# Second feed-forward: blocks run further ahead, the last 512 tokens end chunk by chunk, GpSimd drains early

## The chip, the cores and the metric

The kernel runs on one core of a Trainium2 chip. The core has five engines that run side by side: TensorE (PE in the profile; its weight loads are listed apart as PEld), VectorE (DVE), ScalarE (ACT), GpSimd (POOL) and SyncE (SP). They share an on-chip memory of 128 partitions; TensorE writes into eight banks of a separate accumulation memory, called `bk[0]` to `bk[7]` here, and VectorE and ScalarE read them. The metric is the device time of one execution in microseconds (us), as the median of several runs.

## The reference, cut to what matters

Three layers follow one another: a gated linear attention over 2 x 768 tokens, a mixture of eight experts of which each token takes one, and a second feed-forward with the Mish activation over all 1536 tokens. The change is in the last.

```python
def _moe2_ref(x, w_in, w_out) -> np.ndarray:      # x: 1536 x 384, w_in: 384 x 2048
    h = x @ w_in
    sp = np.where(h > 20.0, h, np.log1p(np.exp(np.minimum(h, 20.0))))
    g = h * np.tanh(sp)
    return (g @ w_out).astype(np.float32)
```

## The kernel before, in words

The kernel keeps its tokens sorted by expert. In the second feed-forward the 2048 hidden features are 16 groups of 128 (`m` from 0 to 15) and the tokens three groups of 512 (`w0` of 0, 512, 1024). One pair of the two is a **block** `(w0, wd, m)`. For a block, `f1` makes the first product in one bank, `sigma` and `cosine` turn it on ScalarE into the Mish factor (sigmoid, arctangent, sine), `gated` on VectorE multiplies and splits the result into a high part `gh` and a low part `gl`, and `f2` makes the second product. Every product is made of three matmuls (high by high, low by high, high by low), so `f1` is 9 matmuls of 512 columns (3 slices of the 384 inputs) and `f2` 12 matmuls of 384 columns: three for each **chunk** of 128 tokens, summed up over `m` in that chunk's bank. Bank 0, 1, 4 and 5 take first products in turn (`h2_rot`), banks 2, 3, 6 and 7 the sums of four chunks (`o_rot`).

The blocks stand in the list `steps`: a **first pass** with `m` below `MA` = 10 for all three token groups (blocks 0 to 29) and a **second pass** with the other six (from block 30). At the end of a group in the first pass `f_keep` copies the four sums to memory; at its end in the second pass `f_out` adds the kept sum on VectorE, and `f_scatter` puts an indirect DMA on GpSimd's queue that writes the chunk's 128 rows to their places in the output. There are twelve such scatters. Earlier in the program GpSimd issues 24 more indirect DMAs, twelve into a table of tokens (`tab`) and twelve into their order (`toks`), so 36 in all.

The order on each engine is the order of the code. One round of the main loop is `f_head(n)` (the first product of block n; then in `f_mish` ScalarE's work on it, the adds of chunks that are full, and `gated` for the pair of blocks finished a round ago), then `f_tail(n)` (the second product of block n - 3, `LAG2`), then at most one scatter. ScalarE works on two blocks at a time so that it loads its function tables twice a pair. In the last token group of the kernel before, `m` = 15 is split into two halves of 256 tokens, with a pairing of its own, and the last two blocks' second products are interleaved:

```python
        elif i >= len(steps) - 2:

            b, w0 = steps[-3], steps[i][0] // 128
            tail = [(b, w0), (b, w0 + 1), (steps[i], w0), (steps[i], w0 + 1)]
            if i == len(steps) - 1:
                tail[1:3] = tail[2:0:-1]
            for b, c in tail:
                f2(b, [c])
                if full:
                    f_out(full.pop()[1])
                    f_scatter(1)
```

`gh` and `gl` lie side by side in a buffer from `big_tile` (three buffers in turn). The weights of the second feed-forward lie as `whi` and `wlo` in the pools `wr_p[0]` (`m` from 0 to 7) and `wr_p[1]` (the rest), eight buffers of each tag in each pool.

When the last block is out, each engine reads a flag (`slow_i`, L1324), branches past a slow path (L1325), GpSimd waits for its scatters to land and updates their semaphores (INC_SWDGE_SEM), and all engines meet after a drain (L1543).

Of the kernel before, what the change touches and what calls it, by code (L numbers as in the profile page):

```python
# [11 lines left out]
F32R = mybir.dt.float32r  # L12
# [11 lines left out]
def kernel(  # L24
# [18 lines left out]
    nc = tc.nc  # L43
    ctx.enter_context(tc.manual_schedule())
    B, H, S, D = q.shape
    NT, DM = out.shape
# [13 lines left out]
    MF2 = FF2 // 128  # L60
# [4 lines left out]
    PW = 768  # L65
    ATT = 4
    W2N = 512
# [12 lines left out]
    wr_p = {0: main.enter_context(tc.tile_pool(name="wr0", bufs=8))}  # L80
# [71 lines left out]
    MA = 10  # L152
# [23 lines left out]
    whi, wlo, wst_t, cvt_t = {}, {}, {}, {}  # L176
# [163 lines left out]
    def w_second(e, m):  # L340
        i = NP1 * e + m // 2 * 2 + 1
        return [w[i][:, m % 2 * DM:(m % 2 + 1) * DM] for w in (whi, wlo)]


    with ExitStack() as actx:
# [626 lines left out]
        i = NTILE - 1  # L972
# [32 lines left out]
    def big_tile():  # L1005
        return fp.tile([128, 1024], F32, tag="big", name="big", bufs=3)
# [94 lines left out]
        nc.vector.tensor_reduce(out=pk, in_=po, axis=AX.X, op=ALU.add)  # L1101
        nc.vector.tensor_tensor(out=pos_i, in0=pk, in1=rs_all, op=ALU.add)

    g_t, o_t, h2_t, p_t, g_b = {}, {}, {}, {}, [None]
    h2_rot, o_rot = [0, 1, 4, 5], [2, 3, 6, 7]
    h2_n, o_n = [0], [0]

# [31 lines left out]
    def gated(b):  # L1139
        w0, wd, m = b  # L1140
        g = p_t.pop(b)
        if w0 % W2N == 0:
            g_b[0] = big_tile().bitcast(F32R)
        gh, gl = (g_b[0][:, o + w0 % W2N:o + w0 % W2N + wd] for o in (0, W2N))
        nc.vector.tensor_tensor(out=g, in0=g, in1=h2_t.pop(b), op=ALU.mult)  # L1145
        nc.vector.tensor_copy(out=gh, in_=g)
        nc.vector.tensor_tensor(out=gl, in0=g, in1=gh.bitcast(F32), op=ALU.subtract)  # L1147
        g_t[b] = (gh, gl)

    def f2(b, chunks=None):  # L1150
        w0, wd, m = b
        gh, gl = g_t[b]
        wh, wl = w_second(E, m)
        for c in range(w0 // 128, (w0 + wd) // 128) if chunks is None else chunks:
            if m in (0, MA):
                o_t[c] = bk[o_rot[o_n[0] % len(o_rot)]][:, 0:DM]
                o_n[0] += 1
            ts = slice(c * 128 - w0, (c + 1) * 128 - w0)
            for n, (a, b_) in enumerate(((gh, wh), (gh, wl), (gl, wh))):
                nc.tensor.matmul(  # L1160
                    out=o_t[c], lhsT=a[:, ts], rhs=b_,
                    start=(m in (0, MA) and n == 0), stop=(m in (MA - 1, MF2 - 1) and n == 2),
                )
            if m in (MA - 1, MF2 - 1):
                full.append((m, c))

    acc_c, ready, full = {}, [], []
# [14 lines left out]
    def f_out(c):  # L1182
        ob = acc_c.pop(c)
        nc.vector.tensor_tensor(out=ob, in0=o_t.pop(c), in1=ob, op=ALU.add)  # L1184
        ready.append((c, ob))

    def f_scatter(n):
        for c, ob in ready[:n]:
            scatter(out, srt[:, c:c + 1], ob, NT, "out")
        del ready[:n]  # L1190

    steps = []
    for ms in (range(MA), range(MA, MF2)):
        for w0 in range(0, NT, W2N):
            for m in ms:
                wd = W2N // 2 if w0 + W2N == NT and m == MF2 - 1 else W2N
                steps += [(w0 + o, wd, m) for o in range(0, W2N, wd)]
    LAG2 = 3
    NS = len(steps)
    pairs_ = [(n, n + 1) for n in range(0, NS - 3, 2)] + [(NS - 3,), (NS - 2, NS - 1)]  # L1200
    last_of = {p[-1]: p for p in pairs_}
    due = []

    def at(n):
        return steps[n] if 0 <= n < NS else None


    def f_mish(n):
        late = (n - EARLY) // 2 if n > EARLY else -9
        if n % 2 == 0:  # L1210
            late_high(late - 1)
            sigma(at(n)) if at(n) else None
            late_size(late)
        elif at(n):
            sigma(at(n))
        if n in last_of:
            bs = [at(i) for i in last_of[n]]
            cosine(bs)
        for m, c in full:
            (f_out if m >= MA else f_keep)(c)  # L1220
        full.clear()
        now = list(due)
        due.clear()
        if n in last_of:
            due.extend(bs)
        for b in now:
            gated(b)
        if n % 2:
            late_low(late - 2)
            late_join(late - 1)  # L1230
            late_load(late + LATE_AHEAD - 1)
        conv_to(E * MF - EARLY + n + 3 + LEAD)

    def f_head(n):
        if at(n):
            f1(at(n))
        f_mish(n)

    def f_tail(n):
        i = n - LAG2  # L1240
        if 0 <= i < len(steps) - 3:
            f2(steps[i])
        elif i >= len(steps) - 2:

            b, w0 = steps[-3], steps[i][0] // 128
            tail = [(b, w0), (b, w0 + 1), (steps[i], w0), (steps[i], w0 + 1)]
            if i == len(steps) - 1:
                tail[1:3] = tail[2:0:-1]
            for b, c in tail:
                f2(b, [c])  # L1250
                if full:
                    f_out(full.pop()[1])
                    f_scatter(1)

    EARLY = LAG2
    CVT_END = 45
# [57 lines left out]
        late_load(i)  # L1314
    f_mish(EARLY)
    f_tail(EARLY)
    for n in range(EARLY + 1, NS + LAG2):
        f_head(n)
        f_tail(n)
        f_scatter(1)  # L1320


    main.close()
    slow = nc.values_load(slow_i[0:1, 0:1], min_val=0, max_val=1)  # L1324
    with tc.If(slow > 0), ExitStack() as sctx:  # L1325
# [71 lines left out]
        for i in range(NTILE):  # L1397
            b, c = divmod(i, NC_B)
# [149 lines left out]
```

## Time and profile before

| | |
|---|---|
| runs | 444.93, 441.98, 444.04 us; median 444.04 us |
| the profiled execution | 442.65 us, of it 440.8 us from the first to the last instruction (the span) |
| TensorE matmul busy | 416.6 us (95% of the span) |
| weight loads / VectorE / ScalarE / GpSimd busy | 377.8 / 326.2 / 331.6 / 61.1 us |
| mean granted TensorE clock | 0.988 of full speed |

All times in the rows below are microseconds from the start of the span unless marked ns. A matmul's duration in the profile includes its way through the pipeline; the distance between the starts of two matmuls is what one costs in a row of them.

### The profile page before, as it was taken

What the parts mean: (1) busy time and instruction counts of PE and PEld (TensorE: products, weight loads), DVE (VectorE), ACT (ScalarE), POOL (GpSimd) and SP (SyncE); (2) the same over time, 40 slices, a digit from 0 to 9 for tenths busy, and PEclk for the clock granted to TensorE, in tenths of its full rate; (3) what the DMA queues carried; (4) which work ended last, traced back from release to release, by engine and by line L of the source; (5) the groups of instructions that cost most, each with busy time, mean ns of one, the idle gap of its engine ahead of it and who ended that gap; (6) DMA issues with size and microseconds to landing.
All of it is one profiled execution on the core that took longest, in us unless ns stands there. A gap on an engine that the chain in (4) does not pass through costs nothing. (4 is left out here: it accounts for less than half of the span.)

```text
span 440.8 us, 8448 instructions
## 1 busy us (share of the span) xinstructions
PE 416.6 (95%) x3139; PEld 377.8 (86%) x3139; DVE 326.2 (74%) x652; ACT 331.6 (75%) x584; POOL 61.1 (14%) x74
## 2 busy tenths in 40 slices
PE   6899989799999999999999999999999999999990
PEld 2787877589999999999988989899899898998980
DVE  7899997689899979988747857967786544543750
ACT  4877995478878777867688788788788677677760
POOL 3143565210100102100000000000000000030302
PEclk9999999899999999999999999999999999999996
DMA  7999752499999999998842121121000000010102
GB/s 233 351 315 351 262 178 76 158 296 263 319 336 339 317 291 290 341 314 249 243 137 66 43 72 36 37 61 49 1 1 0 1 0 0 1 72 1 71 4 75
DMA packets 51566, 68.89 MB, mean 156 GB/s; under 512 B 5500, under 2 KB 41852, under 8 KB 51516
## 3 DMA queue, kind: packets, MB, share of 16 engines
q1 hardware_dynamic: 49596, 63.55, 46.6%
q0 software_dynamic: 1920, 4.73, 3.0%
q8 instruction: 26, 0.43, 0.4%
q14 instruction: 24, 0.20, 0.1%
HBM read 56.65 MB, written 11.61 MB: 155 GB/s over the span
## 5 line engine op out<-in xcount | busy, mean ns | idle before, releaser
L1160 PE MATMUL bk<-whi,big 128*128 128x384 f32 x384 | 106.5, 338 | 1.4 <-DVE x2l L1066 0.8
L329 DVE TENSOR_TENSOR wlo<-st,whi 128x768 fp32r<-128x768 f32 x74 | 69.9, 953 | 17.7 <-ACT whi L323 17.0
L1145 DVE TENSOR_TENSOR p<-p,bk 128x512 f32<-128x512 f32 (+1 forms) x49 | 33.0, 673 | 58.8 <-ACT p L1137 56.1
L1160 PEld LDWEIGHTS bk<-whi,big 128*128 128x128 f32 x384 | 70.5, 188 | 4.5 <-DVE x2l L1066 1.1
L323 ACT ACTIVATE whi<-st 128x768 fp32r<-128x768 f32 x74 | 61.7, 843 | 6.6 <-DMA st<-in_w_dram 6.5
L1160 PE MATMUL bk<-wlo,big 128*128 128x384 f32 x192 | 64.9, 338 | 0.0
L1131 ACT ACTIVATE p<-bk 128x512 f32<-128x512 f32 (+1 forms) x49 | 28.8, 591 | 39.5 <-PE bk L1119 38.2
L1056 PE MATMUL bk<-hl,whi 128*128 128x240 f32 x192 | 52.9, 276 | 0.0
L1056 PE MATMUL bk<-hh,wlo 128*128 128x240 f32 x192 | 52.7, 275 | 0.0
L1056 PE MATMUL bk<-hh,whi 128*128 128x240 f32 x192 | 52.7, 274 | 0.0
L101 POOL DMA_INDIRECT out_dram<-acc,srt x12 | 11.7, 973 | 236.7 <-DVE acc L1184 234.3
L1119 PE MATMUL bk<-x2l,whi 128*128 128x512 f32 (+1 forms) x147 | 41.8, 393 | 0.0
L1119 PE MATMUL bk<-x2h,wlo 128*128 128x512 f32 (+1 forms) x147 | 41.4, 390 | 0.0
L1119 PE MATMUL bk<-x2h,whi 128*128 128x512 f32 (+1 forms) x147 | 41.2, 389 | 0.0
L1160 PEld LDWEIGHTS bk<-wlo,big 128*128 128x128 f32 x192 | 36.0, 188 | 1.7
L1056 PEld LDWEIGHTS bk<-hl,whi 128*128 128x128 f32 x192 | 36.3, 189 | 0.2 <-DVE hl L1044 0.2
L1056 PEld LDWEIGHTS bk<-hh,whi 128*128 128x128 f32 x192 | 36.4, 189 | 0.0
L1056 PEld LDWEIGHTS bk<-hh,wlo 128*128 128x128 f32 x192 | 36.3, 189 | 0.0
L1043 ACT ACTIVATE hh<-bk 128x240 fp32r<-128x240 f32 x64 | 23.5, 366 | 15.5 <-PE bk L1039 15.2
L1039 PE MATMUL bk<-xh,whi 128*128 128x240 f32 x192 | 33.5, 283 | 1.2 <-DVE hl L1044 1.0
L1147 DVE TENSOR_TENSOR big<-p,big 128x512 fp32r<-128x512 f32 (+1 forms) x49 | 33.4, 682 | 1.7
L1119 PEld LDWEIGHTS bk<-x2h,wlo 128*128 128x128 f32 x147 | 27.3, 187 | 6.7
(222 smaller groups left out, 866.1 us busy)
## 6 DMA issues: line engine op xcount, KB each, us to landing
st<-in_w_dram SPq DMA_DIRECT2D x64, 384.0 KB
qn<-in_q_t_dram SPq DMA_DIRECT2D x12, 256.0 KB
kn<-in_k_t_dram SPq DMA_DIRECT2D x12, 256.0 KB
w<-in_w_in_dram SPq DMA_DIRECT2D x6, 512.0 KB
w<-in_w_out_dram SPq DMA_DIRECT2D x6, 512.0 KB
tab<-zero SPq DMA_DIRECT2D x4, 720.0 KB
an<-in_alpha_t_dram SPq DMA_DIRECT2D x11, 256.0 KB
vn<-in_v_n_dram SPq DMA_DIRECT2D x12, 192.0 KB
```

The source lines that it names most:

```text
L101: r = nc.gpsimd.indirect_dma_start(out=dst[:, :], out_offset=bass.IndirectOffsetOnAxis(ap=idx, axis=0), in_=src, in_offset=None, bounds_ch ...
L323: nc.scalar.activation(out=whi[i], in_=w, func=AF.Copy)
L329: nc.vector.tensor_tensor(out=wlo[i], in0=w, in1=whi[i].bitcast(F32), op=ALU.subtract)
L1039: nc.tensor.matmul(out=hps, lhsT=a[:, kk], rhs=b_[:, kk, :], start=(n == 0), stop=(n == 3 * KD - 1))
L1043: nc.scalar.activation(out=hh, in_=hps, func=AF.Relu)
L1056: nc.tensor.matmul(out=y[n], lhsT=a[:, ns], rhs=b_, start=(m == 0 and t == 0 and n % 2 == 0), stop=(m == MF - 1 and t == 2), skip_group_ch ...
L1119: r = nc.tensor.matmul(out=hps, lhsT=a[:, kk], rhs=b_[:, kk, w0:w0 + wd], start=(n == 0), stop=(n == 3 * KD - 1))
L1131: nc.scalar.activation(out=p, in_=h2_t[b], func=AF.Sigmoid, scale=-1.0)
L1145: nc.vector.tensor_tensor(out=g, in0=g, in1=h2_t.pop(b), op=ALU.mult)
L1147: nc.vector.tensor_tensor(out=gl, in0=g, in1=gh.bitcast(F32), op=ALU.subtract)
L1160: nc.tensor.matmul(out=o_t[c], lhsT=a[:, ts], rhs=b_, start=(m in (0, MA) and n == 0), stop=(m in (MA - 1, MF2 - 1) and n == 2),)
```

## The change

It is confined to the second feed-forward's loop. The split of the last `m` goes: there are 48 blocks, all of 512 tokens, paired two by two. From block 34 on `f_tail` lets the second products fall behind by one more block at a time (three times in all), so the lag goes from three blocks to six; each time there is a round without a second product. For blocks of the second pass `gh` and `gl` go into buffers of `wr_p[0]` instead of `big_tile`. After the loop a new function `f_last` makes the second products of the last six blocks (the last token group's whole second pass), ordered by chunk. Two calls `nc.gpsimd.drain()` are added, after rounds 28 and 44.

```diff
     def gated(b):
         w0, wd, m = b
         g = p_t.pop(b)
-        if w0 % W2N == 0:
-            g_b[0] = big_tile().bitcast(F32R)
-        gh, gl = (g_b[0][:, o + w0 % W2N:o + w0 % W2N + wd] for o in (0, W2N))
+        if m >= MA:
+            gh, gl = (wr_p[0].tile([128, PW], F32R, tag=t, name=t)[:, 0:wd] for t in ("whi", "wlo"))
+        else:
+            t = big_tile().bitcast(F32R)
+            gh, gl = t[:, 0:wd], t[:, W2N:W2N + wd]
...
-            for m in ms:
-                wd = W2N // 2 if w0 + W2N == NT and m == MF2 - 1 else W2N
-                steps += [(w0 + o, wd, m) for o in range(0, W2N, wd)]
+            steps += [(w0, W2N, m) for m in ms]
...
+    NL = MF2 - MA
+    NS2 = MA * NT // W2N
+    assert NS % 2 == 0 and NL % 2 == 0 and NL > LAG2
+    pairs_ = [(n, n + 1) for n in range(0, NS, 2)]
...
+    done2 = [0]
+
     def f_tail(n):
...
+        lag = LAG2 + min(max(n - NS2 - 1, 0) // 3, NL - LAG2)
+        if done2[0] <= n - lag:
+            f2(steps[done2[0]])
+            done2[0] += 1
+
+    def f_last():
+        assert done2[0] == NS - NL
+        last = steps[NS - NL:]
+        cs = range(last[0][0] // 128, (last[0][0] + W2N) // 128)
+
+        def part(bs, c, end=False):
+            for b in bs:
                 f2(b, [c])
-                if full:
-                    f_out(full.pop()[1])
-                    f_scatter(1)
+            if end:
+                f_out(full.pop()[1])
+                f_scatter(1)
+
+        for c in cs[:3]:
+            part(last[:-2], c)
+        for c in cs[:2]:
+            part(last[-2:-1], c)
+        for c in cs[:2]:
+            part(last[-1:], c, True)
+        part(last[-2:], cs[2], True)
+        part(last, cs[3], True)
...
-    for n in range(EARLY + 1, NS + LAG2):
+    for n in range(EARLY + 1, NS):
         f_head(n)
         f_tail(n)
         f_scatter(1)
+        if n in (NS - 20, NS - 4):
+            nc.gpsimd.drain()
+    f_mish(NS)
+    f_scatter(NT // 128)
+    f_last()
```

What this does to the order, at three places. On TensorE around round 34 of the kernel before (`bk4` and `bk5` take the first products of blocks 34 and 35, `bk2` is a chunk's sum; `big_4684` and `big_4688` hold the gated blocks 30 and 31):

```order
L1160 MATMUL bk7_90<-whi75_3868,big_4684 128x384
L1119 MATMUL bk4_87<-x2h_1364,whi78_4356 128x512 x3
L1119 MATMUL bk4_87<-x2l_1365,whi78_4356 128x512 x3
L1119 MATMUL bk4_87<-x2h_1364,wlo78_4357 128x512 x3
L1160 MATMUL bk2_85<-whi75_3868,big_4688 128x384
L1160 MATMUL bk2_85<-wlo75_3869,big_4688 128x384
```

and at the same place of the changed kernel:

```order
L1162 MATMUL bk7_90<-whi75_3868,wlo_4686 128x384
L1119 MATMUL bk4_87<-x2h_1364,whi78_4356 128x512 x3
L1119 MATMUL bk4_87<-x2l_1365,whi78_4356 128x512 x3
L1119 MATMUL bk4_87<-x2h_1364,wlo78_4357 128x512 x3
L1119 MATMUL bk5_88<-x2h_1364,whi78_4356 128x512 x3
L1119 MATMUL bk5_88<-x2l_1365,whi78_4356 128x512 x3
L1119 MATMUL bk5_88<-x2h_1364,wlo78_4357 128x512 x3
L1162 MATMUL bk2_85<-whi75_3868,whi_4690 128x384
```

The first product of block 35 follows that of block 34 directly; block 31's second product comes behind both. The same happens at rounds 37 and 40.

On TensorE near the end of the kernel before, where the second product of `m` = 14 (gated block `big_5155`) begins for the last token group, behind that of `m` = 13 (`big_5125`):

```order
L1160 MATMUL bk7_90<-whi77_4150,big_5125 128x384
L1160 MATMUL bk7_90<-wlo77_4151,big_5125 128x384
L1160 MATMUL bk7_90<-whi77_4150,big_5125 128x384
L1160 MATMUL bk2_85<-whi79_4430,big_5155 128x384
L1160 MATMUL bk2_85<-wlo79_4431,big_5155 128x384
L1160 MATMUL bk2_85<-whi79_4430,big_5155 128x384
L1160 MATMUL bk3_86<-whi79_4430,big_5155 128x384
```

and in the changed kernel, where the same product reads `whi_5145` and `wlo_5146`:

```order
L1162 MATMUL bk6_89<-whi77_4150,whi_5097 128x384
L1162 MATMUL bk6_89<-wlo77_4151,whi_5097 128x384
L1162 MATMUL bk6_89<-whi77_4150,wlo_5098 128x384
L1162 MATMUL bk2_85<-whi79_4430,whi_5145 128x384
L1162 MATMUL bk2_85<-wlo79_4431,whi_5145 128x384
L1162 MATMUL bk2_85<-whi79_4430,wlo_5146 128x384
L1162 MATMUL bk3_86<-whi79_4430,whi_5145 128x384
```

Ahead of it there now stand the 36 matmuls of `m` = 10 to 13 for three chunks (`bk2`, `bk3`, `bk6`), all behind the last first product; behind it come 36 more, of which the last 18 are all for the fourth chunk, `bk7`.

On VectorE at the end of the kernel before (two half blocks of `m` = 15, then the four last adds):

```order
L1145 TENSOR_TENSOR p_5153<-p_5153,bk5_88 128x256
L1146 CAST big_5204<-p_5153 128x256
L1147 TENSOR_TENSOR big_5204<-p_5153,big_5204 128x256
L1145 TENSOR_TENSOR p_5183<-p_5183,bk0_83 128x256
L1146 CAST big_5204<-p_5183 128x256
L1147 TENSOR_TENSOR big_5204<-p_5183,big_5204 128x256
L1184 TENSOR_TENSOR acc_4719<-bk2_85,acc_4719 128x384
L1184 TENSOR_TENSOR acc_4719<-bk3_86,acc_4719 128x384
L1184 TENSOR_TENSOR acc_4722<-bk6_89,acc_4722 128x384
L1184 TENSOR_TENSOR acc_4722<-bk7_90,acc_4722 128x384
```

and in the changed kernel:

```order
L1186 TENSOR_TENSOR acc_4398<-bk3_86,acc_4398 128x384
L1186 TENSOR_TENSOR acc_4401<-bk6_89,acc_4401 128x384
L1186 TENSOR_TENSOR acc_4401<-bk7_90,acc_4401 128x384
L1147 TENSOR_TENSOR p_5090<-p_5090,bk4_87 128x512
L1148 CAST whi_5145<-p_5090 128x512
L1149 TENSOR_TENSOR wlo_5146<-p_5090,whi_5145 128x512
L1147 TENSOR_TENSOR p_5123<-p_5123,bk5_88 128x512
L1148 CAST whi_5150<-p_5123 128x512
L1149 TENSOR_TENSOR wlo_5151<-p_5123,whi_5150 128x512
L1186 TENSOR_TENSOR acc_4722<-bk2_85,acc_4722 128x384
L1186 TENSOR_TENSOR acc_4722<-bk3_86,acc_4722 128x384
```

The adds of the middle token group (`acc_4398`, `acc_4401`) now stand directly ahead of the last two gated blocks. On GpSimd the twelve scatters keep their order; one drain stands ahead of the first of them and one behind the third.

## Rows read from the trace of the kernel before

**Rows 1.** The page: span, then busy time, share and instructions of each engine.
```profile
span 440.8 us, 8448 instructions
PE 416.6 (95%) x3139; PEld 377.8 (86%) x3139; DVE 326.2 (74%) x652; ACT 331.6 (75%) x584; POOL 61.1 (14%) x74
```

**Rows 2.** Windows of two rounds: busy time per engine, clock, DMA share, GB/s.
```profile
core 0: us, PE busy (x) PEld busy (x) DVE busy (x) ACT busy (x) POOL busy (x), PEclk, DMA share, GB/s
405.40:413.82 8.42, 8.42 (x44) 7.60 (x44) 5.38 (x10) 6.14 (x9) 1.77 (x2) 1.00 0.06 23
```

**Rows 3.** Timeline of TensorE: start, duration, engine, line, operation, tiles, count.
```profile
409.61 0.85 PE L1119 MATMUL bk<-x2h,whi 128*128 128x512 f32 x3
...
411.71 0.34 PE L1160 MATMUL bk<-whi,big 128*128 128x384 f32 x1
...
413.81 0.86 PE L1119 MATMUL bk<-x2h,whi 128*128 128x512 f32 x3
...
425.21 0.34 PE L1160 MATMUL bk<-whi,big 128*128 128x384 f32 x1
426.14 0.44 PE L1160 MATMUL bk<-whi,big 128*128 128x384 f32 x1 [0.59 <-DVE big L1146]
...
429.34 0.33 PE L1160 MATMUL bk<-whi,big 128*128 128x384 f32 x1
```

**Rows 4.** Timeline of VectorE near the end.
```profile
410.92 1.94 DVE L1184 TENSOR_TENSOR acc<-bk,acc 128x384 f32<-128x384 f32 x4
...
416.34 0.46 DVE L1146 CAST big<-p 128x512 fp32r<-128x512 f32 x1
...
418.70 0.69 DVE L1147 TENSOR_TENSOR big<-p,big 128x512 fp32r<-128x512 f32 x1
...
429.71 0.56 DVE L1184 TENSOR_TENSOR acc<-bk,acc 128x384 f32<-128x384 f32 x1 [0.49 <-PE bk L1160]
```

**Rows 5.** Timeline of GpSimd near the end.
```profile
411.74 0.97 POOL L101 DMA_INDIRECT out_dram<-acc,srt  x1 [19.89 <-DVE acc L1184]
...
428.41 0.97 POOL L101 DMA_INDIRECT out_dram<-acc,srt  x1 [11.86 <-DVE acc L1184]
...
432.24 0.97 POOL L101 DMA_INDIRECT out_dram<-acc,srt  x1 [0.30 <-issue]
```

**Rows 6.** Line L101, GpSimd's scatters, ns min/median/max; landings in 428:433.5, then 386:392.
```profile
L101 POOL DMA_INDIRECT toks<-tokid,pos_i x12: 970/980/1752, 96.2 to 183.7; - x12
L101 POOL DMA_INDIRECT out_dram<-acc,srt x12: 972/973/976, 387.0 to 432.2; - x12
...
DMA to landing us min/median/max: 3.5/3.5/3.5
DMA to landing us min/median/max: 2.8/2.8/2.8
```

**Rows 7.** The kernel's end, L1325 and L1543 (q: an engine's sequencer).
```profile
L1325 POOLq EVENT_SEMAPHORE  x3: 43/43/4280, 431.5 to 435.9; - x3
L1325 POOLq INC_SWDGE_SEM  x1: 900/900/900, 436.0 to 436.0; - x1
...
L1543 SPq DRAIN  x2: 7/10/13, 437.6 to 437.7; - x2
L1543 POOLq DRAIN  x1: 3013/3013/3013, 437.0 to 437.0; - x1
...
L1543 POOLq DRAIN  x2: 40/74/107, 440.2 to 440.5; - x2
```

**Rows 8.** The kernel's start, L1536.
```profile
L1536 POOLq INC_SWDGE_SEM  x1: 31/31/31, 0.2 to 0.2; - x1
...
L1536 POOLq DRAIN  x1: 187/187/187, 0.4 to 0.4; - x1
```

**Rows 9.** Weight loads of two lines, whole span: ns min/median/max, first and last start.
```profile
L1160 PEld LDWEIGHTS bk<-whi,big x384: 186/188/189, 233.7 to 429.2; 128*128 128x128 f32 x192
...
L1056 PEld LDWEIGHTS bk<-hh,wlo x192: 187/189/193, 93.8 to 231.5; 128*128 128x128 f32 x192
```

More of the change, by code (lines that the diff above doesn't have):

```diff
@@ L1102, in sort_places @@
         nc.vector.tensor_tensor(out=pos_i, in0=pk, in1=rs_all, op=ALU.add)
-    g_t, o_t, h2_t, p_t, g_b = {}, {}, {}, {}, [None]
+    g_t, o_t, h2_t, p_t = {}, {}, {}, {}
     h2_rot, o_rot = [0, 1, 4, 5], [2, 3, 6, 7]
@@ L1194 @@
         for w0 in range(0, NT, W2N):
-            for m in ms:
-                wd = W2N // 2 if w0 + W2N == NT and m == MF2 - 1 else W2N
-                steps += [(w0 + o, wd, m) for o in range(0, W2N, wd)]
+            steps += [(w0, W2N, m) for m in ms]
     LAG2 = 3
     NS = len(steps)
-    pairs_ = [(n, n + 1) for n in range(0, NS - 3, 2)] + [(NS - 3,), (NS - 2, NS - 1)]
+    NL = MF2 - MA
+    NS2 = MA * NT // W2N
+    assert NS % 2 == 0 and NL % 2 == 0 and NL > LAG2
+    pairs_ = [(n, n + 1) for n in range(0, NS, 2)]
     last_of = {p[-1]: p for p in pairs_}
@@ L1237, in f_head @@
         f_mish(n)
+    done2 = [0]
     def f_tail(n):
[L1240 to L1249, printed above, removed]
-                f2(b, [c])
-                if full:
-                    f_out(full.pop()[1])
-                    f_scatter(1)
+        lag = LAG2 + min(max(n - NS2 - 1, 0) // 3, NL - LAG2)
[8 more added lines that the diff above has]
+            for b in bs:
+                f2(b, [c])
+            if end:
[9 more added lines that the diff above has]
+        part(last, cs[3], True)
     EARLY = LAG2
```

## The prediction

> **What bounds the kernel now.** I read the page first, then windows of a few rounds, then the timelines of the last 30 us and the rows of the program's end. TensorE's matmuls cover 95% of the span [rows 1]. In the stretch that the change rewrites, two rounds of the main loop take 8.42 us and TensorE is busy in all of it at full granted clock, with ScalarE at 6.14 and VectorE at 5.38 us [rows 2]: a round costs two products on TensorE, and nothing there waits for another engine. So matmuls that only change places are worth nothing. What can be won lies where TensorE stops. There are two such places. At 425.2 it waits once for VectorE, and from 429.7 to the end of the span at 440.8 it has no work, and the last adds, the scatters, their landing and the program's close follow one another. The span is 440.8 us and the profiled execution 442.65, so 1.85 us lie around it.
>
> The close reads so. The last add starts at 429.71 and takes 0.56 [rows 4], to 430.27. The last scatter starts only at 432.24, with nothing ahead of it but the three others of its group, 0.97 us each with 0.30 between [rows 5]. It lands 3.5 us after its start [rows 6], at about 435.8. GpSimd's waits end with that, INC_SWDGE_SEM starts at 436.0 and takes 0.90, and at 437.0 a drain begins that takes 3.01 us; SyncE is through its own two drains by 437.7 and then only waits [rows 7]. The span ends 0.8 us after the long drain.
>
> **The stop before the last products.** Before, the second product of `m` = 14 stood right behind that of `m` = 13, and the matmul after the one at 425.21 starts at 426.14, released by the cast [rows 3]. A second product's 12 matmuls take from 411.71 to 413.81, so 0.175 us each. The 18 matmuls from the stop on would have started at 425.39 and the last of them at 425.39 + 17 x 0.175 = 428.36; it starts at 429.34 [rows 3]. The stop and the slower matmuls behind it cost 0.98 us. After the change 36 matmuls (6.3 us) and the second product of block 41 (2.1 us) lie between the last first product and the first need of `m` = 14, which is 8.4 us. The chain through ScalarE and VectorE, read at the pair whose last first product ends at 411.71, has the first block's high part at 416.34 + 0.46, or 5.1 us later, and the second block's low part at 418.70 + 0.69, or 7.7 us later [rows 3, 4]; that one is needed 6 matmuls and a bit further on, at about 9.8. The cover is 2 to 3 us, so I count the whole 0.98 as won. The four adds of the middle group now stand ahead of these two blocks on VectorE. They take 1.94 us [rows 4] and begin as the second product of block 41 fills its chunks, 0.5 us after TensorE starts it; they end about 2.7 us after the last first product, while VectorE's part of the pair begins with a multiply some 0.7 us ahead of that cast, 3.9 us after it, so they delay nothing.
>
> **The queue of scatters.** The last chunk's 18 matmuls (3.2 us) now stand alone behind the third chunk's last one, and the third ends 1.05 us behind the second. Scatters follow one another in 1.27 us [rows 5], so the three before are issued within 4 us of the first add and GpSimd is idle when the fourth add ends. The first add of the middle group, of four in 1.94 us from 410.92, ends near 411.47, and its scatter starts at 411.74 [rows 4, 5]: 0.27 us. Before, the last scatter started 432.24 - 430.27 = 1.97 us behind its add. Won: 1.70. Together with the stop the last scatter starts 2.68 us earlier, at 429.56. The middle group's four scatters are issued while `f_last` runs its first 36 matmuls and are off the queue over 3 us before the last group's first add.
>
> **The landing.** I leave it at the 3.5 us of the last scatter; the middle of the pass shows 2.8 [rows 6], which would win 0.7 more. 3.5 is the nearer row, since the program's close, with its code and flag reads on the other engines, lies beside both. The Trainium skill (DMA: Bandwidth & Descriptors, section on the anatomy of one DMA) fits such a DMA as 2.0 us plus its bytes at 436 GB/s. For 128 rows of 384 floats that would be an estimate of 2.45 us, and the time below would be 1.05 lower; both rows of this trace are above it.
>
> **The drains.** No early drain is in the trace, so its worth is bounded. The long drain of 3.01 us comes after 36 indirect DMAs; the two behind it take 0.107 and 0.040 [rows 7], and one at the start, with the same INC_SWDGE_SEM ahead of it but no DMA, 0.19 [rows 8]. So a drain leaves nothing for the next, and the semaphore instruction alone doesn't make one long: something left over from the DMAs does. If it grows with their number it is (3.01 - 0.11) / 36 = 0.081 us each. The first new drain stands behind 24 of them, the second behind 3, and 9 are left: 0.11 + 9 x 0.081 = 0.83 us, which wins 2.18. If instead any DMA makes a drain long, the nine suffice, and nothing is won. I take the first, because the two short drains show that what is left over is used up. SyncE sets a floor: its drains end at 437.7, and GpSimd's would end at 437.0 + 0.83 = 437.8, so nearly all of it counts. The new drains themselves are counted at nothing. The first has the 202 us between the last `toks` scatter at 183.7 and the first output scatter at 387.0 [rows 6] as its cover. Behind the second only the fourth chunk's scatter is queued; GpSimd idled 19.89 us between the first and the second group of scatters [rows 5], and no buffer waits for that one. A drain there would have to take over 15 us to matter.
>
> **What costs nothing else.** The split of the last `m` had the same columns as the block that replaces it, and ScalarE, which saves some instructions there, is not late. The three rounds without a second product shift TensorE's work within an unbroken row. Such a pair of rounds takes 8.42 - 2.10 = 6.32 us of TensorE against ScalarE's 6.14 [rows 2, 3]; ScalarE keeps up, and should it not, a first product needs a bank only after the block four before it is gated, which leaves about 4 us. The buffers of `wr_p[0]` hold weights last read in the first pass, and eight blocks fit where at most six or seven are alive.
>
> **The sum.** 0.98 + 1.70 + 2.18 = 4.86 us. Against the profiled execution this is 442.65 - 4.86 = 437.8 (a span of 435.9). That execution lies below the median of 444.04; the three runs and it average 443.4, and from this level I predict 443.4 - 4.86 = **438.5**. One per cent, about what a measurement here can tell from no change, is 4.4 us.
>
> **Rivals.** First, **the last drain stays long**, that is, the change doesn't do there what it says. For it: one drain can't tell a fixed price from one per DMA. Against it: the short drains. Only 2.68 is won, 440.7. Second, **more than the drain shrinks**: INC_SWDGE_SEM took 0.03 with nothing behind it and 0.90 with 36 DMAs [rows 7, 8]; if it goes by their number too, nine give 0.03 + 0.87 x 9 / 36 = 0.25, 0.65 less, and a last scatter alone in flight may land in 2.8, 0.7 less. That gives 437.2; against it speaks that SyncE's waits may not move with it. Third, **TensorE waits somewhere new**: ScalarE has 0.18 us to spare in each of the three short pairs. If its pair took 7.4 us there instead of 6.14, the three would be 3.3 us late in all, and what the banks don't absorb would come back as stops; at the worst 441.8. The rows show no gap on ScalarE that large. Fourth, the one that ends slower, **dearer second products**: the 18 blocks of the second pass, 216 matmuls, load their stationary operand from `wr_p[0]`, the same kind of buffer from which their moving operand comes. It decides from 4.86 / 216 = 22 ns a matmul on; at 45 ns, a quarter of one, the time would be 443.4 - 4.86 + 9.7 = 448.2. Against it: loads take 186 to 193 ns both from `big_tile` and, in the experts' second products (L1056), from the weight pools [rows 9], and at 5 ns the loss is 1.1 us.
>
> **How the numbers follow.** The forecast gets 0.54, the long drain 0.25, the larger gain 0.12, new waits 0.05, dearer products 0.04. The forecast's own range is 437.3 to 439.7. The whole range goes down to 436.6 (the second rival less half a microsecond) and up to 441.9: 440.7 and 1.2 more, most of the 1.5 by which the slowest run lay above the mean. More than 1% faster needs a gain of 4.4, half a microsecond under the forecast: 0.6 of 0.54, nearly all of 0.12 and little of the rest make 0.45. Slower by over 1% is most of the last rival, 0.03, and the remaining 0.52 is within 1%.
>
> **What the new profile would show.** Right: no idle time of TensorE from 310 to its last matmul, which starts near 428.4; the last scatter within 0.4 us of the last add's end; two drains on GpSimd in mid program that nobody waits for, and a last drain under a microsecond; SyncE and GpSimd ready within 0.3 us of each other. Wrong: a last drain near 3 us (then look at what follows the second early drain), a TensorE wait on a bank or on a gated block after round 34, a scatter slower than 1 us beside VectorE's casts, or a second product's matmul further apart than 0.176 us. The surest way to be wrong is the price of the drain, on which nearly half of the sum rests.

## The result and the profile after

| | before | after |
|---|---|---|
| median | 443.76 us (4 runs, 441.98 to 444.93) | 437.79 us (4 runs, 436.88 to 438.31) |
| ratio, 95% interval | | 0.9881, 0.9852 to 0.9911 |
| profiled execution, its span | 442.65, 440.8 | 437.65, 435.8 |

The kernel became 1.2% faster; the forecast was 438.5. One run of the repeated changed kernel (the last of the experiments), 441.54 us, lay over 1.5% above that kernel's fastest and is left out of its median. The page of the changed kernel stands beside [rows 1]:

```profile
span 435.8 us, 8410 instructions
PE 415.6 (95%) x3125; PEld 378.1 (87%) x3130; DVE 326.4 (75%) x649; ACT 328.2 (75%) x579; POOL 61.4 (14%) x74
```

TensorE is 1.0 us less busy and the span is 5.0 us shorter, so most of the gain is time in which TensorE has no work. To see where, I cut the span at the start of block 34's first product. That is 364.19 us after (shown below), and before:

```profile
363.35 0.85 PE L1119 MATMUL bk<-x2h,whi 128*128 128x512 f32 x3
```

What lies ahead of this place has hardly been touched by the change (145.2 us from block 0's first product to block 34's in both), yet block 34 starts anywhere from 361.0 to 365.7 us in the profiled executions of this study. From there to the span's end it is 440.8 - 363.35 = 77.45 us before and 435.8 - 364.19 = 71.6 after: 5.9 us gained, against 6.0 between the medians and 5.3 by the ratio. All sizes below are measured from this place.

The timeline of TensorE after (columns as in [rows 3]) has the first of the three pairs of first products in a row (blocks 34 and 35), the last first product, the first matmul that needs the gated `m` = 14, and the last matmul:

```profile
364.19 0.85 PE L1119 MATMUL bk<-x2h,whi 128*128 128x512 f32 x3
...
366.28 0.86 PE L1119 MATMUL bk<-x2h,whi 128*128 128x512 f32 x3
...
412.21 0.85 PE L1119 MATMUL bk<-x2h,whi 128*128 128x512 f32 x3
...
422.45 0.33 PE L1162 MATMUL bk<-whi,wlo 128*128 128x384 f32 x1
422.62 0.33 PE L1162 MATMUL bk<-whi,whi 128*128 128x384 f32 x1
...
428.69 0.34 PE L1162 MATMUL bk<-whi,wlo 128*128 128x384 f32 x1
```

Between 422.45 and 422.62 nothing is waited for. The waits of the same stretch (engine and line that waits, what it waits for: us in total, times, the longest) name no TensorE at all, and ScalarE waits for TensorE there, not the other way round:

```profile
POOL out_dram L101 <- DVE acc L1186: 230.4, 6, 207.7
...
ACT p L1131 <- PE bk L1119: 21.7, 12, 2.2
```

VectorE's timeline shows why. The four adds of the middle group end at 417.1, then VectorE still waits 1.06 us for ScalarE. `m` = 14 is ready at 419.63 (high part) and `m` = 15 at 422.20 (low part), while `m` = 14 is first read at 422.62 and that low part eight matmuls later, near 424.0:

```profile
415.02 2.12 DVE L1186 TENSOR_TENSOR acc<-bk,acc 128x384 f32<-128x384 f32 x4 [1.23 <-PE bk L1162]
418.20 0.69 DVE L1147 TENSOR_TENSOR p<-p,bk 128x512 f32<-128x512 f32 x1 [1.06 <-ACT p L1137]
418.92 0.71 DVE L1148 CAST whi<-p 128x512 fp32r<-128x512 f32 x1
...
421.51 0.69 DVE L1149 TENSOR_TENSOR wlo<-p,whi 128x512 fp32r<-128x512 f32 x1
...
429.06 0.56 DVE L1186 TENSOR_TENSOR acc<-bk,acc 128x384 f32<-128x384 f32 x1 [2.57 <-issue]
```

GpSimd's timeline has the four last scatters in two pieces. The fourth starts 0.28 us behind the end of its add (429.06 + 0.56 = 429.62), where it was 1.97 [rows 4, 5]:

```profile
425.21 0.97 POOL L101 DMA_INDIRECT out_dram<-acc,srt  x1 [4.55 <-DVE acc L1186]
...
427.77 0.97 POOL L101 DMA_INDIRECT out_dram<-acc,srt  x1 [0.30 <-issue]
429.90 0.97 POOL L101 DMA_INDIRECT out_dram<-acc,srt  x1 [1.16 <-DVE acc L1186]
```

The rows of the program's end answer to [rows 7]; the last line is the two new drains (ns min/median/max, first and last start):

```profile
L1346 POOLq INC_SWDGE_SEM  x1: 364/364/364, 433.8 to 433.8; - x1
...
L1564 POOLq DRAIN  x3: 46/107/784, 434.1 to 435.5; - x3
L1564 SPq DRAIN  x3: 7/7/13, 434.8 to 435.2; - x3
...
L1338 POOLq DRAIN  x2: 4631/6725/8819, 182.7 to 393.0; - x2
```

Both short forms of the close are there: INC_SWDGE_SEM 0.364 us for 0.900, and the last drain (the one that had been long) 0.784 for 3.013. In one table, from block 34's first product on (us):

| term | before | after | gained | forecast |
|---|---|---|---|---|
| to the start of the last matmul | 65.99 | 64.50 | 1.5 | 0.98 |
| end of the last add to the last scatter | 1.97 | 0.28 | 1.69 | 1.70 |
| last scatter to INC_SWDGE_SEM (landing and waits) | 3.8 | 3.9 | -0.1 | 0 |
| INC_SWDGE_SEM | 0.90 | 0.36 | 0.54 | 0 |
| last drain | 3.01 | 0.78 | 2.23 | 2.18 |

The sum is 5.9. The last matmul to the last add, and the last drain to the end of the span, take the same in both.

### The profile page after: what moved, and what is told of

It is laid out like the page before. It is cut to its first block, busy times and chain, and to the rows that moved or that the text cites. A ratio compares the mean times of both kernels' runs of the same rounds, so it can differ in the third digit from the quotient of the medians.

```text
span 435.8 us, 8410 instructions
## 1 busy us (share of the span) xinstructions
PE 415.6 (95%) x3125; PEld 378.1 (87%) x3130; DVE 326.4 (75%) x649; ACT 328.2 (75%) x579; POOL 61.4 (14%) x74
## 4 chain that ended last, share of the span: by engine, by line
PE 73%; DVE 14%; ACT 3%; issue 3%; DMA 3%; POOL 1%; SPq 0%; ACTq 0%; POOLq 0%; DVEq 0%
PE bk L1162 22%; PE bk L1119 22%; PE bk L1039 11%; PE bk L1056 10%; DVE wlo L329 4%; DMA w<-in_w_out_dram 2%; PE bk L506 2%; PE bk L552 2%; DVE pt L444 1%; PE bk L570 1%; DMA qn<-in_q_t_dram 1%; DVE hl L1044 1%; PE bk L773 1%; PE bk L1011 1%; DVE er L471 1%
## 5 line engine op out<-in xcount | busy, mean ns | idle before, releaser
L1147 DVE TENSOR_TENSOR p<-p,bk 128x512 f32<-128x512 f32 x48 | 32.8, 683 | 51.8 <-ACT p L1137 51.8
L1162 PE MATMUL bk<-whi,big 128*128 128x384 f32 x240 | 66.6, 338 | 0.8 <-DVE x2l L1066 0.8
L1131 ACT ACTIVATE p<-bk 128x512 f32<-128x512 f32 x48 | 28.8, 599 | 35.2 <-PE bk L1119 33.6
L1162 PEld LDWEIGHTS bk<-whi,big 128*128 128x128 f32 x240 | 44.1, 188 | 2.6 <-DVE x2l L1066 1.1
L101 POOL DMA_INDIRECT out_dram<-acc,srt x12 | 11.9, 992 | 234.5 <-DVE acc L1186 230.4
L1119 PE MATMUL bk<-x2l,whi 128*128 128x512 f32 x144 | 41.7, 397 | 0.0
L1119 PE MATMUL bk<-x2h,wlo 128*128 128x512 f32 x144 | 41.2, 394 | 0.0
L1119 PE MATMUL bk<-x2h,whi 128*128 128x512 f32 x144 | 41.0, 393 | 0.0
L1162 PE MATMUL bk<-wlo,big 128*128 128x384 f32 x120 | 40.6, 338 | 0.0
L1119 PEld LDWEIGHTS bk<-x2l,whi 128*128 128x128 f32 x144 | 27.1, 188 | 6.3
L1137 ACT ACTIVATE p<-p,quarter 128x512 f32<-128x512 f32 x48 | 32.1, 717 | 0.3
```

Source lines behind the costliest of these rows:

```text
L101: r = nc.gpsimd.indirect_dma_start(out=dst[:, :], out_offset=bass.IndirectOffsetOnAxis(ap=idx, axis=0), in_=src, in_offset=None, bounds_ch ...
L1119: r = nc.tensor.matmul(out=hps, lhsT=a[:, kk], rhs=b_[:, kk, w0:w0 + wd], start=(n == 0), stop=(n == 3 * KD - 1))
L1131: nc.scalar.activation(out=p, in_=h2_t[b], func=AF.Sigmoid, scale=-1.0)
L1137: nc.scalar.activation(out=p_t[b], in_=p_t[b], func=AF.Sin, scale=-2.0, bias=quarter)
L1162: nc.tensor.matmul(out=o_t[c], lhsT=a[:, ts], rhs=b_, start=(m in (0, MA) and n == 0), stop=(m in (MA - 1, MF2 - 1) and n == 2),)
```

## The experiments

Theories: **count** (the price of the last drain grows with the indirect DMAs since the drain before it) against **presence** (any DMA makes it long); and for the half microsecond that TensorE gained beyond its stop (the one wait before its last products), **place** (where the gated blocks lie) against **depth** (eight buffers where there were three) and against more matmuls in a row. Ratios are to the kernel before, run on the same chip alongside.

**Without the two early drains** (changed kernel):

```diff
-        if n in (NS - 20, NS - 4):
-            nc.gpsimd.drain()
```

> The changed kernel without its two early drains. If what a drain has to clear grows with the indirect DMAs issued since the last one, the drain at the program's end has 36 behind it again: near 3.0 us instead of 0.78, INC_SWDGE_SEM near 0.90 instead of 0.36, together 2.8 us more, so about 440.5 us against 437.8 with the drains. Rival, the last drain was long because four scatters were issued back to back just before it: with the scatters spread out it stays under 1 us without the early drains too, and the time stays at 437.8.

Measured: 438.45 us (10 runs), ratio 0.9923 (0.9897 to 0.9948). The rows of its end:

```profile
L1344 POOLq INC_SWDGE_SEM  x1: 900/900/900, 432.0 to 432.0; - x1
...
L1562 POOLq DRAIN  x3: 40/107/3013, 432.9 to 436.5; - x3
```

Both are back at their length of before, to the nanosecond. From block 34 (362.73) to the span's end (436.8) it is 74.1 us, 2.5 more than in the changed kernel. Its TensorE time is the changed kernel's: the last matmul starts at 427.22, 64.49 us behind block 34.

**Only the first of the two drains**, so that 12 DMAs are left:

```diff
-        if n in (NS - 20, NS - 4):
+        if n == NS - 20:
```

> The changed kernel with the drain after round 28 alone, so that 12 indirect DMAs and not 9 are left for the last drain. By number (0.78 less 0.11 over 9 is 0.075 us each): last drain 0.11 + 12 x 0.075 = 1.01 us and INC_SWDGE_SEM about 0.42, a loss of 0.3 us, not to be told from the changed kernel in the time but in the rows. Rival, a drain's length goes by the time or the work since the last one, or is fixed once any DMA came after it: then it lies between 1.3 and 3 us, or at 0.78.

Measured: 436.61 us (4 runs), ratio 0.9861 (0.9825 to 0.9898).

```profile
L1346 POOLq INC_SWDGE_SEM  x1: 420/420/420, 433.4 to 433.4; - x1
...
L1564 POOLq DRAIN  x3: 46/107/1039, 433.8 to 435.4; - x3
```

Between nine and twelve DMAs the drain grows by 0.255 us and INC_SWDGE_SEM by 0.056, as the count theory had it; presence would have left both as they were in the changed kernel. From block 34 to the end it is 71.6 us in both, since in this execution the last scatter's landing was 0.3 us shorter (429.84 to 433.4).

**The kernel before with the two drains alone**, at the places in its own loop that leave nine DMAs too:

```diff
         f_scatter(1)
+        if n in (28, 41):
+            nc.gpsimd.drain()
```

> The kernel before with nothing but two early drains, after round 28 and behind the third output scatter; order of products and scatters as before. If the drains work alone, the last drain is 0.78 us, INC_SWDGE_SEM 0.36, and the time 2.8 us under that of the kernel before, about 441.0. Rival, they need the spread scatters: the last drain stays over 2 us and the time within 1 us of 443.8.

Measured: 439.01 us (8 runs), ratio 0.9911 (0.9884 to 0.9937). INC_SWDGE_SEM takes 0.360 and the last drain 0.784 us, with the last scatter still 1.96 us behind its add and the last matmul 66.0 us behind block 34:

```profile
L1327 POOLq INC_SWDGE_SEM  x1: 360/360/360, 436.6 to 436.6; - x1
...
L1545 POOLq DRAIN  x3: 46/107/784, 437.0 to 438.3; - x3
```

To the end of the span it is 75.0 us, 2.5 less than before: the two instructions give 2.77, and the last landing took 0.3 longer here. The drains need nothing of the rest of the change.

**Three drains**, the third ahead of `f_last`, so that four DMAs are left:

```diff
     f_scatter(NT // 128)
+    nc.gpsimd.drain()
     f_last()
```

> The changed kernel with a third drain, on GpSimd between the middle token group's four scatters and the last group's, where GpSimd idles 4.5 us. By number 4 DMAs are left: last drain 0.11 + 4 x 0.083 = 0.44 us, INC_SWDGE_SEM 0.26 instead of 0.36. But SyncE's waits start only as INC_SWDGE_SEM ends and take 0.8 us, so the end moves by no more than 0.16 us: 437.6. Rival, without SyncE's floor the whole 0.34 + 0.10 us would be won: 437.35. The rows decide.

Measured: 435.47 us (4 runs), ratio 0.9869 (0.9797 to 0.9941). The last drain takes 0.376 us and INC_SWDGE_SEM 0.260:

```profile
L1347 POOLq INC_SWDGE_SEM  x1: 260/260/260, 431.6 to 431.6; - x1
...
L1565 POOLq DRAIN  x3: 46/107/376, 431.9 to 433.1; - x3
L1565 SPq DRAIN  x3: 7/7/13, 432.5 to 432.8; - x3
```

The drain ends 0.41 us sooner after its start, but the rest of the span behind it takes 1.18 instead of 0.84 us: the program's end now waits for SyncE. Of 0.51 us in GpSimd's two instructions 0.17 is left, as was expected. From block 34 to the end it is 71.3 us, 0.3 less than in the changed kernel, because the landing was 0.12 shorter as well.

**The second drain moved to just ahead of the last scatter**:

```diff
-        if n in (NS - 20, NS - 4):
+        if n == NS - 20:
...
+        nc.gpsimd.drain()
         part(last, cs[3], True)
```

> The changed kernel with its second drain moved to the place just ahead of the very last scatter, where GpSimd idles 1.2 us. If a drain waits until the DMAs before it have landed (both early drains ended 0.2 to 1.0 us after the last landing before them), the last scatter is held until the one before has landed, some 1.6 to 2.5 us later than now, and little of it comes back from a last drain of 0.19 us: 439.2 to 440.0. Rival, a drain only clears finished entries at 0.08 us each: the idle time hides most of it, and the time is 437.6.

Measured: 437.11 us (4 runs), ratio 0.9894 (0.9831 to 0.9957). The moved drain and the landing of the last scatter ahead of it, the program's end, then the two scatters around the moved drain:

```profile
L1269 POOLq DRAIN  x1: 4575/4575/4575, 424.4 to 424.4; - x1
...
L101 POOL DMA_INDIRECT out_dram<-acc,srt x1: 972/972/972, 425.6 to 425.6; - x1
DMA to landing us min/median/max: 2.9/2.9/2.9
```

```profile
L1347 POOLq INC_SWDGE_SEM  x1: 195/195/195, 433.4 to 433.4; - x1
...
L1565 POOLq DRAIN  x3: 46/107/131, 433.6 to 434.9; - x3
```

```profile
425.59 0.97 POOL L101 DMA_INDIRECT out_dram<-acc,srt  x1 [0.30 <-issue]
429.80 0.97 POOL L101 DMA_INDIRECT out_dram<-acc,srt  x1 [3.24 <-issue]
```

The third scatter of the group starts at 425.59, and the drain, which the sequencer reached at 424.4 while the scatters were still queued, ends at 428.9: it waits until what is in flight has landed (the last of it at 428.45) and takes 0.49 us more. The first early drain shows the same in the five runs whose trace has the landing ahead of it: it took from 7.6 to 9.8 us, and each time ended 1.03 us after that landing. The last add ended at 427.45, so the last scatter starts 2.36 us behind it instead of 0.28. The last drain is down to 0.131 us and INC_SWDGE_SEM to 0.195, but the rest waits for SyncE again (1.42 us), and from block 34 to the end it is 73.1, 1.5 more than after. A drain is free only where the queue has time to land.

**All four chunks end together again** (changed kernel, the order of `f_last` alone):

```diff
-        for c in cs[:3]:
+        for c in cs:
             part(last[:-2], c)
...
-        part(last, cs[3], True)
+        part(last[-2:], cs[3], True)
```

> The changed kernel with another order in f_last alone: all four chunks take the first four blocks, and the last two blocks end the four chunks as in the kernel before, 6 matmuls apart, so that the four last scatters come due within 2 us. If the queue of scatters costs what was forecast, the last scatter starts 1.9 us behind the last add again, and the time is 1.7 us up, 439.5 against 437.8. Rival, the scatters' own queue is hidden behind the landing of the one before, and what moved the end was the stop alone: time unchanged.

Measured: 435.76 us (4 runs), ratio 0.9863 (0.9799 to 0.9928).

```profile
426.18 0.56 DVE L1186 TENSOR_TENSOR acc<-bk,acc 128x384 f32<-128x384 f32 x1 [0.49 <-PE bk L1162]
```

```profile
424.41 0.97 POOL L101 DMA_INDIRECT out_dram<-acc,srt  x1 [6.63 <-DVE acc L1186]
...
428.25 0.97 POOL L101 DMA_INDIRECT out_dram<-acc,srt  x1 [0.30 <-issue]
```

The last scatter starts 1.51 us behind its add. That is 1.23 more than in the changed kernel, but 0.46 less than before, though all four end together in both: before, the first add also had to wait until VectorE was through with the second half of `m` = 15, which bunched the adds. In the timeline of VectorE before:

```profile
425.79 0.29 DVE L1146 CAST big<-p 128x256 fp32r<-128x256 f32 x1
...
427.24 0.42 DVE L1147 TENSOR_TENSOR big<-p,big 128x256 fp32r<-128x256 f32 x1
427.58 1.64 DVE L1184 TENSOR_TENSOR acc<-bk,acc 128x384 f32<-128x384 f32 x3
```

In this execution the landing was 0.5 us shorter than in the changed kernel's (3.34 us from the last scatter's start to INC_SWDGE_SEM instead of 3.85), and from block 34 to the end it is 72.3, 0.7 more. That stretch took from 3.55 to 4.12 us in the runs that keep the changed kernel's order, so a difference of half a microsecond there says nothing. The 1.23 rests on the rows of this one execution; the expected 1.7 us does not show in the time, and the medians can't tell the two kernels apart.

**The kernel before with the new buffers alone**:

```diff
-        if w0 % W2N == 0:
-            g_b[0] = big_tile().bitcast(F32R)
-        gh, gl = (g_b[0][:, o + w0 % W2N:o + w0 % W2N + wd] for o in (0, W2N))
+        if m >= MA:
+            gh, gl = (wr_p[0].tile([128, PW], F32R, tag=t, name=t)[:, 0:wd] for t in ("whi", "wlo"))
+        else:
+            t = big_tile().bitcast(F32R)
+            gh, gl = t[:, 0:wd], t[:, W2N:W2N + wd]
```

> The kernel before with nothing but the gated blocks of the second pass in the weight buffers of wr_p[0]. In the changed kernel a second product's 12 matmuls take 2.085 us from block 31 on, against 2.109 before. If the place of the operand does that, this kernel shows 2.085 from block 31 on too, and with 17 blocks gains some 0.5 us, 443.3. Rival, the lag of the second products behind the first does it (an operand that has long been written): then 2.109 stays, the stop of 0.6 us before the last products stays, and the time is that of before, 443.8.

Measured: 441.12 us (10 runs), ratio 0.9988 (0.9964 to 1.0013). A round, and the stop, in TensorE's timeline:

```profile
376.74 0.34 PE L1162 MATMUL bk<-whi,whi 128*128 128x384 f32 x1
...
378.83 0.85 PE L1119 MATMUL bk<-x2h,whi 128*128 128x512 f32 x3
...
383.00 0.85 PE L1119 MATMUL bk<-x2h,whi 128*128 128x512 f32 x3
...
424.47 0.45 PE L1162 MATMUL bk<-whi,whi 128*128 128x384 f32 x1 [0.59 <-DVE whi L1148]
...
427.64 0.34 PE L1162 MATMUL bk<-whi,wlo 128*128 128x384 f32 x1
```

The 12 matmuls of a second product take 378.83 - 376.74 = 2.09 us for 2.10 [rows 3], a round 4.17 for 4.21 (8.42 / 2, [rows 2]). The stop is still there, and the medians can't show half a microsecond. From block 34 (362.13) to the last matmul it is 65.51: the new buffers are worth 65.99 - 65.51 = 0.48 us, and doing away with the stop 65.51 - 64.49 = 1.02 (64.49 from the kernel without the drains). These two kernels also differ in the split of the last `m`, whose two halves' first products take 2.12 us for the 2.09 of one whole block, so some 0.03 of the 1.02 is the split's.

**The kernel before with three of the new buffers used in turn**, as many as `big_tile` has:

```diff
+            if len(three) < 3:
+                three.append([wr_p[0].tile([128, PW], F32R, tag=t, name=t) for t in ("whi", "wlo")])
+            gh, gl = (t[:, 0:wd] for t in three[three_n[0] % 3])
+            three_n[0] += 1
```

> The kernel before with the gated blocks of the second pass in buffers of wr_p[0], as in the run with the buffers alone, but in three of them in turn, as deep as the ring that they had. If it is the place of the operand that shortens the matmuls, a second product's 12 matmuls stay at 2.085 us. Rival, it is the depth of the ring (a buffer written again only eight blocks later, and no wait or signal for it): then they go back to 2.109. The whole time differs by 0.4 us between the two, too little to tell; the rows decide.

Measured: 442.30 us (10 runs), ratio 1.0006 (0.9976 to 1.0035). The round stays short, so it is the place and not the depth:

```profile
378.18 0.85 PE L1120 MATMUL bk<-x2h,whi 128*128 128x512 f32 x3
...
382.35 0.85 PE L1120 MATMUL bk<-x2h,whi 128*128 128x512 f32 x3
...
386.52 0.85 PE L1120 MATMUL bk<-x2h,whi 128*128 128x512 f32 x3
...
390.83 0.85 PE L1120 MATMUL bk<-x2h,whi 128*128 128x512 f32 x3
```

Two of its rounds are 0.14 us longer than the others (the one from 386.52 is shown): there a weight load waits 0.3 us for VectorE's adds, a wait that the run with eight buffers does not have. With a slightly longer stop this gives back most of the 0.48 (the last matmul starts 65.92 us behind block 34).

**The place, used for the first pass too.** Three kernels, run side by side. The first keeps the third drain and gives `big_tile` a pool of its own, ahead of the weight pools:

```diff
+    bgp = main.enter_context(tc.tile_pool(name="bgp", bufs=3))
...
-        return fp.tile([128, 1024], F32, tag="big", name="big", bufs=3)
+        return bgp.tile([128, 1024], F32, tag="big", name="big", bufs=3)
```

> The changed kernel with the third drain, and with the three buffers of big_tile in a pool of their own ahead of the weights' second pool, so at another place of the on-chip memory, for the first pass too. If the place of big_tile's buffers makes the matmuls of a round longer, the first pass's second products (30 blocks) now take 2.085 us instead of 2.109 and its first products 2.088 instead of 2.098: 30 x 0.034 = 1.0 us less than with the third drain alone. Rival, it is something else about those buffers (their width, the high and the low part side by side in one): then the first pass stays at 2.109 and the time at that of the run with three drains.

The second, with the third drain too, moves the whole pool `fp`, in which `big_tile` lies, ahead of the pool of `x2h` and `x2l`, so that these now lie behind it:

```diff
+    fp = main.enter_context(tc.tile_pool(name="fp", bufs=2))
+    fpool[0] = fp
...
-    fp = main.enter_context(tc.tile_pool(name="fp", bufs=2))
-    fpool[0] = fp
```

> The changed kernel with the third drain, and with the pool of big_tile placed ahead of the second feed-forward's inputs x2h and x2l, which so lie at the end of the memory in its stead. If it is the end of the memory that is slow to read for whoever lies there, second products of the first pass go to 2.085 us and first products, which now read x2l there, get longer than 2.098. Rival, only the distance or the place relative to other buffers counts: second products change, first products don't; or nothing changes at all, 2.109 and 2.098.

The third is the changed kernel again:

> The changed kernel once more, beside the two versions of this call, so that they can be compared with it and not only with the kernel before. The same kernel as measured: 0.988 of the time before; rows from the first product of block 34 to the end 71.6 us.

Measured: 436.07 us (6 runs), ratio 0.9834 (0.9794 to 0.9875); 436.05 (4 runs), 0.9863 (0.9808 to 0.9918); 436.55 (5 runs), 0.9850 (0.9808 to 0.9892). A round of the first pass in the timeline of TensorE, with the pool of its own:

```profile
300.87 0.85 PE L1120 MATMUL bk<-x2h,whi 128*128 128x512 f32 x3
...
305.04 0.85 PE L1120 MATMUL bk<-x2h,whi 128*128 128x512 f32 x3
```

and in the changed kernel run beside it:

```profile
303.50 0.86 PE L1119 MATMUL bk<-x2h,whi 128*128 128x512 f32 x3
...
307.71 0.85 PE L1119 MATMUL bk<-x2h,whi 128*128 128x512 f32 x3
```

The round is 4.17 us instead of 4.21. From block 0's first product to block 34's it is 144.26 us instead of 145.24, and 144.33 in the second kernel. The rows give the pool of its own 1.0 us there and 0.2 more by the third drain; the medians, 0.5 apart with intervals that overlap, don't separate it from the changed kernel. By the rows these two kernels, equal but for the last landing (3.55 and 4.12 us), are the best of this study. In the second kernel first products did not get longer, though `x2l` now lies at the end, behind `fp`:

```profile
302.56 0.85 PE L1119 MATMUL bk<-x2h,whi 128*128 128x512 f32 x3
...
304.65 0.34 PE L1162 MATMUL bk<-whi,big 128*128 128x384 f32 x1
```

That is 2.09 us. So what counts is the place of the gated tiles, and not that of the moving operands. A second product loads the gated tiles as its weights and VectorE writes them; which of the two the place slows down is not shown, and a first product, which reads none of them, also went from 2.098 to 2.088 us in the run with the new buffers alone. Why the place matters stays open; no run here changes the address alone.

## Why the prediction was right

**The bound.** Right. TensorE's row is unbroken through the three short rounds; what was won lies at its stop and behind its last matmul, but for half a microsecond.

**The stop.** Right, with one misreading. It is gone, and was worth 1.02 us (forecast 0.98) by the two kernels that differ in it. But it did not stand before `m` = 14, as the prediction took it: the six matmuls of `m` = 14 for two chunks end with the one at 425.21, and the cast that TensorE waited for (425.79, 256 columns) is that of the first half of `m` = 15. The sum is untouched, since the 18 matmuls behind the stop were counted rightly. The cover was 3.0 us for `m` = 14 (ready 419.63, read 422.62) and 1.8 for the low part of `m` = 15 (ready 422.20, read near 424.0), near the forecast's 2 to 3, and the moved adds delayed nothing.

**The queue of scatters.** Right in size, 1.69 for 1.70. The run with the four chunks together splits it: 1.23 by the order of the chunks, 0.46 because the last adds are no longer bunched behind a late gated block. The prediction gave all of it to the order; that the sum of the two met its 1.70 is because it read the gap itself off the rows.

**The landing.** Kept, rightly: the last scatter lands 3.6 us after its start where [rows 6] had 3.5, though nearly alone in flight. The 0.7 that the second rival hoped for here did not come. The reason that the prediction gave, code and flag reads at the program's close, no run tests. The Trainium skill's fit (DMA: Bandwidth & Descriptors, section on the anatomy of one DMA), an estimate of 2.45 us for this DMA, is below it; in the run with the first drain alone, whose trace has all 36 landings, the shortest took 2.6 us, the median 3.5.

**The drains.** The count, on which nearly half the sum rested, was right, and the first rival, that the last drain stays long, is refuted: 0.83 us was forecast with nine DMAs left, and 0.784 measured. The other runs make a line of it:

| indirect DMAs since the last drain | 1 | 4 | 9 | 12 | 36 |
|---|---|---|---|---|---|
| last drain, us | 0.131 | 0.376 | 0.784 | 1.039 | 3.013 |
| INC_SWDGE_SEM, us | 0.195 | 0.260 | 0.364 | 0.420 | 0.900 |

From 1 to 36 the drain grows by 2.88 us in 35 steps, 0.082 us each (forecast 0.081). It does not go by bytes: all 36 write 128 rows, and the step is the same between 12 and 36, where twelve of them write 4 bytes a row, as below 12, where all write 1536. Whether it goes by DMAs or by rows can't be told here. In mid program the price is half of that. Counted from the last landing ahead of it to its end, an early drain took:

| indirect DMAs since the last drain | 3 | 5 | 11 | 24 |
|---|---|---|---|---|
| early drain after the last landing, us | 0.16 | 0.24 | 0.49 | 1.03 |

These are 0.041 us a DMA; why the close pays double is open. SyncE's floor was right too. It is reached at nine DMAs, where the two are ready together; below that the saving is lost to the wait for SyncE. That the new drains cost nothing was right in the time, but not because they are short: they take 8.8 and 4.6 us, and nothing waits for what stands behind them. Behind the second that is the first token group's fourth scatter, which started 2.56 us after the third's end instead of 0.30.

**Mis-sized: INC_SWDGE_SEM.** That this instruction stays as long as it was is the one step about the close that failed. It was left at 0.90 in the sum and given to the second rival at 0.25. It goes by the number of DMAs as well, 0.020 us each (0.705 in 35 steps) upon 0.18 (with none it took 0.03 [rows 8]), and took 0.36: 0.54 us that the sum lacked. The doubt that SyncE's waits would not move with it did not hold at nine DMAs: in all thirteen profiles SyncE was through its two drains 0.76 us after INC_SWDGE_SEM's end.

**Missed: the pace of the matmuls.** The fourth rival asked whether second products from `wr_p[0]` are dearer, and found the loads alike [rows 9]. The loads are alike, but the matmuls behind them come 2.085 us for 12 where they took 2.109 from `big_tile`, and the round's first product is 0.01 us shorter too. That is 0.48 us won over the rest of the pass, with the sign opposite to that rival's.

**New waits** (third rival) did not come: ScalarE waited for TensorE throughout. So the sum was 4.86 and the gain 5.9; INC_SWDGE_SEM's 0.54 and the pace's 0.48 are the difference. That the median came out only 0.7 below the forecast is because the kernel before, counted at 443.4, stood at 443.76.

## What to carry to other kernels

A program that has queued many indirect DMAs on GpSimd pays for their number when it closes; a drain put earlier, where the queue has microseconds to land and nobody stands behind it, takes that price off the end, until another engine's close is the floor. In mid program each DMA costs half as much. At the end of a program what counts is how little is left behind the last matmul: let the pieces finish one by one, with the last one's work behind the others' transfers, and give the producers of the last operands enough independent matmuls as cover. To find terms of half a microsecond, measure from a fixed place near the change to the end, since what lies ahead of it can vary by more between executions.

## What the runs showed of the hardware

- A GpSimd drain first waits until the indirect DMAs in flight have landed (8.8, 4.6 and 4.6 us in mid program, waits included). For each DMA since the drain before it, it then takes 0.04 us in mid program and 0.08 at the program's close, where INC_SWDGE_SEM takes 0.02 for each besides.
- Where the gated blocks lay changed a second product's 12 matmuls from 2.109 to 2.085 us and a first product's 9 from 2.098 to 2.088, with no wait on any engine, in buffers of the weight pools, with three or eight of them, and of a pool of their own alike. The block whose second product is the first to read the new place still took 2.115.
